# A fused convolution and feed-forward kernel on one core: another order for the same 923 operations

## The chip, the core and the metric

The kernel runs on one NeuronCore of a Trainium2 chip. Five engines work from queues of their own, each strictly in order: TensorE (PE; its weight loads are PEld), VectorE (DVE), ScalarE (ACT), GpSimd (POOL) and SyncE (SP). SP issues transfers only; POOL issues transfers and does small arithmetic. The transfers run on 16 DMA engines that all queues share. The metric is device time in microseconds (us), lower is better.

## The reference

```python
def _A_ref(q, k, v, shift_k, ssm_k, ssm_D):
    ...
    for t in range(ks):                       # 4 taps along the sequence
        k_shift = k_shift + k_pad[:, t:t + S, :] * shift_k[:, ks - 1 - t][None, None, :]
    kv = k_shift * v
    ...                                       # causal convolution of kv with ssm_k by FFT
    y = y + kv * ssm_D[None, None, :]
    return q * y

def _B_ref(x, w_gate, w_up, w_down):
    g = _silu(x @ w_gate)
    u = x @ w_up
    return (g * u) @ w_down

x = A_q
h = x + _A_ref(_layernorm(x, axis=-1), A_k, A_v, A_shift_k, A_ssm_k, A_ssm_D)
h2 = h + _B_ref(_layernorm(h, axis=-1), B_w_gate, B_w_up, B_w_down)
```

The sequence has 2048 positions, the model width is 640, the feed-forward width is 1728, and everything is bfloat16.

## The kernel before

The sequence is cut into four blocks (0 to 3) of 512 positions. The long convolution is done block by block in a frequency domain, and each transform is a set of matrix products. Per block the stages are:

- **Loads.** The filter block g (line 289, from `A_ssm_k`), k (lines 404 and 477), v (line 296), x (line 301, from `A_q`); in block 0 also the transform matrices `WF` (line 903) and `WI` (line 909), the taps (line 889) and the skip weights (line 904).
- **Turning.** g and k are needed with the channels and positions exchanged. Block 0 does it on TensorE (line 411, evicted from PSUM by line 413); later blocks do it with transposing transfers on SP (line 404), for g after a rearranging copy on ScalarE (line 419).
- **kv.** The four taps are small matrix products (line 490); VectorE multiplies by v (line 513 in block 0, line 515 later).
- **Spectra.** Products with `WF` (line 329), evicted from PSUM by line 319 on ScalarE, then sums and differences on VectorE (lines 361 to 396).
- **Products of spectra.** Block j multiplies the spectra X of blocks 0 to j with filter windows H and adds them up: products on VectorE (line 542), sums on VectorE (line 545) or by *adding transfers*, in which the DMA engines read one SBUF tile and add it into another (line 243). Block 3 has the most of these: products with four windows.
- **Inverse.** Sums on VectorE (lines 662 to 677), products with `WI` (line 698), the first layernorm's scale (line 707), gating with x (line 709), the second layernorm's sums (line 606), `rstd` on POOL (line 610).
- **Turning h.** Row tiles (line 722 on ScalarE or 724 on VectorE), turned on TensorE (line 411) or by SP.
- **Feed-forward.** Gate and up products (line 769), silu (line 783), then either a copy on ScalarE (line 785) with a product on VectorE (line 787), or one product on VectorE straight from PSUM (line 786); down products (line 845), and the result added to `out` by an adding transfer (line 852) or stored (lines 754 and 866).

The feed-forward of block j-1 is listed beside the convolution of block j, so that TensorE has matrix products while VectorE works on spectra. Block 3's feed-forward has nothing beside it and runs last.

**What sets the order.** Python code first lists all 923 operations with their reads and writes (`Plan.add`). Then `Plan.run` emits them in the sequence that the hand-given table `ORDER` states (lines 47 to 92), checking that the inputs of each were emitted before. An engine's queue is thus the table, filtered to that engine. A number n stands for operation n; a negative number -n-1 stands for operation n in its second form, on another engine. The forms are these:

```python
evict: ScalarE copy        -> VectorE copy
added: VectorE tensor_add  -> nc.gpsimd.dma_start(..., accum_op=ALU.add)
load:  nc.sync.dma_start   -> nc.gpsimd.dma_start
```

Tiles of the large SBUF arena (22 units) and the four PSUM slots are handed out as `run` goes along, so the table also decides which buffer an operation gets and what it must wait for.

The completion semaphores of transfers are eight per kind of queue, used in turn: the ninth transfer of a queue waits for the landing of the first.

Of the kernel before, what the change touches and what calls it, by code (L numbers as in the profile page):

```python
# [44 lines left out]
UNITS = 22  # L45
SLOTS = {"row": 5, "sg": 3, "ps": 4, "sm": 10}
ORDER = (
# [42 lines left out]
WHOLE = ((0, 1),)  # L90
HB = BLK // 2
DCUTS = ((0, 5), (5, 10), (10, NC_FULL))
# [898 lines left out]
```

## Time and profile before

| what | value |
|---|---|
| time, median of 3 runs | 251.96 us (250.69 to 254.26) |
| profiled execution, span from first to last instruction | 251.4 us |
| median of the runs above the profiled span | 0.56 us |
| PE busy | 237.3 us (94%) |
| DVE busy | 197.7 us (79%) |
| ACT busy | 173.9 us (69%) |
| POOL busy | 54.0 us (21%) |
| DMA queue of SP (hardware_dynamic) | 21.38 MB, 32.1% of the 16 engines' time |
| DMA queue of POOL (software_dynamic) | 11.96 MB, 25.9% |
| granted TensorE clock | 1.000 |

For the profiled execution the page gives the span and no other time; the timed runs are separate executions. "Busy" is the time in which an instruction was executing. The rows quoted in the prediction come from views of the profile: the page itself, the table of stretches of time, the lists of waits, the timeline, the groups by line, and the transfers. In a wait's row the three numbers are total us, times, longest us. In the timeline and in the chain of waits they are start and duration in us. Times of all views are counted from the span's start.

### The profile page before, as it was taken

To read this page: it belongs to the slowest core of one execution; us is meant where nothing else is said; L and a number is where in the kernel's file an instruction comes from. 1 tells how busy PE (TensorE), PEld (TensorE's weight loads), DVE (VectorE), ACT (ScalarE), POOL (GpSimd) and SP (SyncE) were. 2 spreads that over 40 slices of the span, in tenths; PEclk is the share of its full clock that TensorE was granted. 3 is DMA by queue.
4 is the path that set the end of the run, shared out by engine and by line. 5 is a ranking of instruction groups with operands and counts; after the bars stand their busy time and mean duration, and the time that the engine had idled before them with its cause. 6 is when DMAs were issued, how large, how long until landed. Compare 5 with 4: busy or idle time off the path is not lost.

```text
span 251.4 us, 5138 instructions
## 1 busy us (share of the span) xinstructions
PE 237.3 (94%) x2113; PEld 153.0 (61%) x2125; DVE 197.7 (79%) x249; ACT 173.9 (69%) x300; POOL 54.0 (21%) x54
## 2 busy tenths in 40 slices
PE   3869997999999999999999999999999999999994
PEld 3447675788777677444465676454456785465662
DVE  2379999999999999999999989999999542131222
ACT  2449998999999976975988789983542865325100
POOL 0002003231540313220270404263612110000030
PEclk9999999999999999999999999999999999999999
DMA  5995699774998654685345468889592200000052
GB/s 156 376 212 163 127 324 352 231 197 92 165 246 292 202 81 81 105 154 133 79 66 146 86 99 194 148 146 163 98 224 29 26 0 3 0 0 3 0 78 78
DMA packets 37283, 33.66 MB, mean 134 GB/s; under 512 B 22470, under 2 KB 32076, under 8 KB 37260
## 3 DMA queue, kind: packets, MB, share of 16 engines
q1 hardware_dynamic: 31884, 21.38, 32.1%
q0 software_dynamic: 5376, 11.96, 25.9%
q8 instruction: 16, 0.26, 0.4%
q14 instruction: 7, 0.06, 0.1%
HBM read 16.29 MB, written 4.59 MB: 83 GB/s over the span
## 4 chain that ended last, share of the span: by engine, by line
PE 56%; ACT 17%; DMA 10%; DVE 9%; issue 4%; SPq 3%; DVEq 0%; ACTq 0%; POOLq 0%
PE ps L769 24%; PE ps L845 22%; ACT arena L319 7%; DMA arena<-in_A_ssm_k_dram 7%; PE ps L698 5%; DMA arena<-arena 3%; ACT sg L785 2%; PE ps L490 2%; SPq L404 2%; ACT junk L606 1%; PE ps L329 1%; PE ps L833 1%; DVE arena L674 1%; DVE arena L663 1%; DVE arena L662 1%
## 5 line engine op out<-in xcount | busy, mean ns | idle before, releaser
L769 PE MATMUL ps<-arena,wgu 128*128 128x512 bf16 (+1 forms) x668 | 116.7, 328 | 1.4 <-ACT sg L809 0.5
L769 PEld LDWEIGHTS <-wgu 128*128 128x128 bf16 x680 | 66.2, 98 | 45.3 <-issue 1.4
L845 PE MATMUL ps<-wd,tT 128*128 128x320 bf16 x416 | 59.1, 299 | 0.0
L845 PEld LDWEIGHTS <-tT 128*128 128x128 bf16 x416 | 39.8, 98 | 17.2 <-issue 1.8
L542 DVE TENSOR_TENSOR arena<-arena 128x2560 bf16<-128x2560 bf16 x30 | 44.1, 1484 | 0.2
L783 ACT ACTIVATE sg<-ps 128x1024 bf16<-128x1024 f32 (+1 forms) x28 | 26.9, 968 | 20.3 <-PE ps L769 19.7
L329 PE MATMUL ps<-arena,WF 128*128 128x320 bf16 x176 | 29.8, 299 | 1.2 <-ACT arena L319 0.9
L785 ACT CAST sg<-ps 128x1024 bf16<-128x1024 f32 (+1 forms) x23 | 23.0, 998 | 6.9 <-PE ps L769 3.1
L319 ACT CAST arena<-ps 128x320 bf16<-128x320 f32 (+1 forms) x48 | 25.2, 583 | 1.9 <-DVE arena L545 1.1
L610 POOL TENSOR_TENSOR sm<-sm,neghalf 128x4 f32<-128x4 f32 (+1 forms) x10 | 16.6, 1659 | 43.4 <-DVE sm L646 43.1
L787 DVE TENSOR_TENSOR tT<-sg,sg 128x1024 bf16<-128x1024 bf16 (+1 forms) x23 | 15.5, 673 | 11.5 <-ACT sg L785 11.5
L243 POOL DMA_DIRECT2D arena<-arena x11 | 13.3, 1211 | 47.4 <-DVE arena L542 11.2
L329 PEld LDWEIGHTS <-WF 128*128 128x128 bf16 x176 | 17.1, 98 | 10.0 <-issue 2.3
L606 ACT ACTIVATE junk<-arena 128x640 bf16<-128x640 bf16 x28 | 20.8, 744 | 1.3 <-DVE arena L709 1.3
L545 DVE TENSOR_TENSOR arena<-arena 128x2560 bf16<-128x2560 bf16 x14 | 20.7, 1487 | 0.2
L319 ACT ACTIVATE arena<-ps 128x640 bf16<-128x640 f32 (+1 forms) x32 | 20.2, 655 | 0.3
L698 PE MATMUL ps<-arena,WI 128*128 128x320 bf16 x96 | 15.7, 299 | 0.9 <-issue 0.6
L850 ACT ACTIVATE row<-ps,sm 128x640 bf16<-128x640 f32 x12 | 9.5, 791 | 8.2 <-PE ps L845 8.0
L709 DVE SCALAR_TENSOR_TENSOR arena<-arena,sm,ps 128x640 bf16<-128x640 bf16 x16 | 13.6, 876 | 1.8 <-ACT ps L707 1.8
L852 POOL DMA_DIRECT2D out_dram<-row x12 | 11.7, 1153 | 14.1 <-ACT row L850 14.1
L707 ACT ACTIVATE ps<-ps,sm 128x640 f32<-128x640 f32 x16 | 12.1, 770 | 3.7 <-PE ps L698 3.5
L698 PEld LDWEIGHTS <-WI 128*128 128x128 bf16 x96 | 9.0, 97 | 5.6 <-issue 1.3
(91 smaller groups left out, 240.8 us busy)
## 6 DMA issues: line engine op xcount, KB each, us to landing
arena<-arena POOLq DMA_DIRECT2D x11, 640.0 KB, 6.1
arena<-in_A_q_dram SPq DMA_DIRECT2D x4, 640.0 KB, 5.1
out_dram<-row POOLq DMA_DIRECT2D x13, 160.0 KB, 4.2
arena<-in_A_ssm_k_dram SPq DMA_DIRECT2D x3, 640.0 KB, 9.4
arena<-in_A_v_dram SPq DMA_DIRECT2D x3, 640.0 KB, 6.3
wd<-in_B_w_down_dram SPq DMA_DIRECT2D x2, 800.0 KB, 7.3
out_dram<-arena POOLq DMA_DIRECT2D x2, 640.0 KB, 5.8
wgu<-in_B_w_gate_dram SPq DMA_DIRECT2D x1, 800.0 KB, 6.5
```

What stands on the lines that cost most here:

```text
L319: (lambda: nc.scalar.activation(dst(), src(), ACT.Copy, scale=2.0)) if twice else (lambda: nc.scalar.copy(dst(), src())),
L329: nc.tensor.matmul(ap(ps)[:, h, 0:NH], w, ap(src)[:, r, h * NH:(h + 1) * NH], start=(first and i == 0), stop=(last and i == len(rs) - 1), ...
L542: dve(1402, lambda: v.tensor_mul(to(), X.part(xs), H.part(hs)), [X.at(xs), H.at(hs)], [at])
L545: added(1402 * n - 69 * (n - 1), lambda: v.tensor_add(to(), to(), b()), to, b, [what], at, n)
L606: act(725, lambda r=r: nc.scalar.activation(waste(), ap(x)[:, r, :], ACT.Square, scale=D ** -0.5, accum_out=sm(s, MSQ, (r,))), [(x, r)], [ ...
L610: nc.gpsimd.tensor_tensor(sm(s, RSTD, rs), sm(s, VAR, rs), ap(neghalf)[:, 0:len(rs)], op=ALU.pow)
L698: nc.tensor.matmul(ap(ps)[:, w, 0:NH], m, src[:, w * NH:(w + 1) * NH], start=(i == 0), stop=(i == len(terms) - 1))
L769: nc.tensor.matmul(split(ap(ps), n)[:, i, :], w(k), ap(hT)[:, k, lo:lo + n], start=(k == 0), stop=(k == KT - 1))
L783: act(905 if wide_ else 490, lambda: nc.scalar.activation(of(sg), of(*gate), ACT.Silu), [(gate[0], gate[1] + i) for i in range(m)] + (psu ...
L785: op = plan.add("act", 905 if wide_ else 490, lambda: nc.scalar.copy(of(co), of(*up)), psu + [sg], [co] + tt, ("dve", 1135 if wide_ else 6 ...
L787: op.rest = dve(602 if wide_ else 336, lambda: nc.vector.tensor_mul(to(), of(sg), of(co)), [sg, co], tt)
L845: nc.tensor.matmul(ap(ps[hf])[:, hf, 0:NH], ap(tT)[:, c * BLK + at:c * BLK + at + P], ap(wd)[:, c, hf * NH:(hf + 1) * NH], start=False, st ...
```

## The change

Only the table `ORDER` is replaced; all functions stay as they are and their line numbers too. The same 923 operations come in another sequence, and other ones carry a minus sign. With 11 adding transfers before there are 17 now; of plain loads and stores 5 went through POOL's queue, now 21; of evictions 20 were on VectorE, now 26. In detail, nine sums become adding transfers and three go back to VectorE; nineteen plain transfers come to POOL's queue and three go back to SP; twelve evictions come to VectorE and six go back to ScalarE.

```diff
 ORDER = (
-    0, 1, 2, 3, 16, 18, -20, 5, 4, 8, 17, 186, 9, 20, 22, 7, 10, 11, -22, 24, -26, 23, 26, 75, 76, 13, 15, 12, 6,
...
+    0, 16, -18, 8, -16, 3, 1, 9, 5, 10, 18, -20, 7, 26, 2, 11, -187, 20, 21, -13, 22, 24, 23, -26, 75, 76, 6, -14,
...
```

Three places of the program show what that does to the queues.

**SP's queue at the start.** First its rows before, then its rows now (`arena<-in_A_ssm_k_dram` is a filter block, `arena<-arena` a turning of it, `kT` the turned k).

```order
L477 DMA arena<-in_A_k_dram 128x1280
L889 DMA arena<-in_A_shift_k_dram 5x512
L477 DMA arena<-in_A_k_dram 128x1280
L289 DMA arena<-in_A_ssm_k_dram 128x5x512
L296 DMA arena<-in_A_v_dram 128x2560
L903 DMA WF<-const_wf 128x1024
L904 DMA arena<-in_A_ssm_D_dram 1x640
L289 DMA arena<-in_A_ssm_k_dram 128x5x512
L903 DMA WF<-const_wf 128x1024
L301 DMA arena<-in_A_q_dram 128x2560
L909 DMA WI<-const_wi 128x1024 x2
```

```order
L477 DMA arena<-in_A_k_dram 128x1280
L889 DMA arena<-in_A_shift_k_dram 5x512
L296 DMA arena<-in_A_v_dram 128x2560
L404 DMA_TRANSPOSE arena<-arena 128x5x128
L404 DMA_TRANSPOSE kT<-in_A_k_dram 128x5x128
```

SP keeps half of k, the taps and v; it comes to the turning of block 1's g and k after its third transfer, where before all of block 0's loads stood ahead of that.

**POOL's queue at the start**, as a piece of the difference (the rows without a sign stand in both).

```order
+L477 DMA arena<-in_A_k_dram 128x1280
+L904 DMA arena<-in_A_ssm_D_dram 1x16x40
 L872 ISA
 L872 AFFINE_SELECT ident<-ident 128x128
+L289 DMA arena<-in_A_ssm_k_dram 128x5x512 x2
+L903 DMA WF<-const_wf 128x1024 x2
+L301 DMA arena<-in_A_q_dram 128x2560
+L737 DMA wgu<-in_B_w_gate_dram 128x5x640
 L875 MEMSET neghalf 128x4
+L909 DMA WI<-const_wi 128x1024 x2
+L301 DMA arena<-in_A_q_dram 128x2560
 L624 TENSOR_SCALAR sm_76<-sm_76 128x4
```

Eleven transfers stand now ahead of POOL's first layernorm step (line 624): the first of the two filter blocks is block 1's, the second is block 0's, and the gate weights of line 737 are among them.

**POOL's queue during block 3's products of spectra**, before and then now (line 243 is an adding transfer, 852 an addition to `out`, 754 a store of h to `out`; the rows of lines 634 to 610 are block 3's first layernorm, `sm_83`).

```order
L296 DMA arena<-in_A_v_dram 128x2560
L243 DMA arena<-arena 128x2x1280 x3
L634 TENSOR_TENSOR sm_83<-sm_83 128x4
L635 TENSOR_TENSOR sm_83<-sm_83 128x4
L636 TENSOR_SCALAR sm_83<-sm_83 128x4
L610 TENSOR_TENSOR sm_83<-sm_83,neghalf 128x4
L243 DMA arena<-arena 128x2x1280 x2
L852 DMA out_dram<-row_68 128x640
L243 DMA arena<-arena 128x2x1280
L852 DMA out_dram<-row_64 128x640
L852 DMA out_dram<-row_66 128x640
L852 DMA out_dram<-row_65 128x640
```

```order
L243 DMA arena<-arena 128x2x1280
L852 DMA out_dram<-row_67 128x640
L852 DMA out_dram<-row_68 128x640
L243 DMA arena<-arena 128x2x1280
L852 DMA out_dram<-row_64 128x640
L852 DMA out_dram<-row_65 128x640
L243 DMA arena<-arena 128x2x1280 x6
L634 TENSOR_TENSOR sm_83<-sm_83 128x4
L635 TENSOR_TENSOR sm_83<-sm_83 128x4
L636 TENSOR_SCALAR sm_83<-sm_83 128x4
L610 TENSOR_TENSOR sm_83<-sm_83,neghalf 128x4
```

The products of block 3 have eight adding transfers of 640 KB where they had six, and the layernorm step stands now behind the last of them. One sum of block 3 that was an adding transfer earlier in the program (the sum of filter windows, line 466) is back on VectorE.

82 rows, old and new, of the table ORDER are left out of this document.

## The prediction

> **What bounds the kernel now.** I read the totals first, then the table of stretches, then TensorE's waits and its timeline in the stretch that has holes.
>
> ```profile
> span 251.4 us, 5138 instructions
> ...
> PE 237.3 (94%) x2113; PEld 153.0 (61%) x2125; DVE 197.7 (79%) x249; ACT 173.9 (69%) x300; POOL 54.0 (21%) x54
> ```
>
> TensorE (PE) is busy for 237.3 of 251.4 us, so 14.1 us of its idle time are all that an order could ever win. The table of stretches says where they lie (after the stretch's length: busy us of each engine and its instructions, the granted clock, the DMA engines' busy share, GB/s):
>
> ```profile
> core 0: us, PE busy (x) PEld busy (x) DVE busy (x) ACT busy (x) POOL busy (x), PEclk, DMA share, GB/s
> 0.00:15.00 15.00, 7.93 (x174) 5.25 (x175) 5.80 (x16) 4.68 (x4) 0.54 (x6) 1.00 0.94 281
> 15.00:31.00 16.00, 15.97 (x124) 11.26 (x125) 14.92 (x30) 15.28 (x41) 1.88 (x2) 1.00 0.69 137
> 31.00:45.00 14.00, 12.19 (x218) 8.38 (x218) 13.75 (x25) 12.47 (x26) 2.04 (x1) 1.00 1.04 335
> 45.00:68.00 23.00, 22.50 (x204) 19.34 (x203) 22.57 (x21) 22.94 (x40) 6.96 (x5) 1.00 0.69 159
> 68.00:248.00 180.00, 178.72 (x1395) 108.82 (x1406) 140.12 (x160) 118.53 (x193) 42.53 (x41) 1.00 0.51 105
> 248.00:251.40 3.40, 0.00 (x0) 0.00 (x0) 0.53 (x1) 0.00 (x0) 0.00 (x0) 1.00 0.08 24
> ```
>
> The reader is to see 7.1 us of idle PE in the first 15, 1.8 between 31 and 45, 0.5 up to 68, 1.3 in the next 180, and 3.4 after the last product. The granted clock is 1.00 throughout. From 68 us on, PE is the bound, and saving work on another engine there wins nothing. Between 15 and 31 PE counts as busy, but ScalarE (15.28) and VectorE (14.92) are about as full: small products and their evictions keep step.
>
> PE's waits (total us, times, longest) and its timeline at the start name the holes:
>
> ```profile
> PE ps L411 <- DMA arena<-in_A_k_dram: 4.0, 1, 4.0
> PE ps L411 <- DMA arena<-in_A_ssm_k_dram: 3.0, 1, 3.0
> PE ps L329 <- ACT arena L319: 0.9, 1, 0.9
> ```
>
> ```profile
> 6.58 2.44 PE L490 MATMUL ps<-diag,kT 32*128 32x128 bf16 x112
> 8.95 2.68 PE L882 MATMUL ps<-ident 128*128 128x512 bf16 x9
> 11.55 0.43 PE L490 MATMUL ps<-diag,kT 32*128 32x128 bf16 x28
> 14.96 1.03 PE L411 MATMUL ps<-ident,arena 128*128 128x128 bf16 x15 [2.98 <-DMA arena<-in_A_ssm_k_dram]
> 15.82 0.82 PE L329 MATMUL ps<-arena,WF 128*128 128x320 bf16 x4
> ...
> 45.23 1.03 PE L769 MATMUL ps<-arena,wgu 128*128 128x256 bf16 x8 [0.16 <-ACT arena L413]
> ```
>
> PE gets k at 4.0, works until 11.98, and waits 3.0 us for block 0's filter, which lands at 14.91 (row of the chain of waits below). The first spectrum product (line 329) starts at 15.82, the first feed-forward product (line 769) at 45.23.
>
> **The start.** What the loads do together, in two windows, and the chain's row:
>
> ```profile
> 3.90 11.01 DMA arena<-in_A_ssm_k_dram
> ```
>
> ```profile
> DMA packets 2621, 4.22 MB, mean 281 GB/s; under 512 B 391, under 2 KB 1677, under 8 KB 2620
> ...
> q1 hardware_dynamic: 2620, 4.20, 93.2%
> ```
>
> ```profile
> DMA packets 2077, 3.30 MB, mean 367 GB/s; under 512 B 354, under 2 KB 1389, under 8 KB 2076
> ```
>
> The first answer is for 0 to 15 us, the second for 6 to 15. In before all loads stand in SP's queue and the filter lands only when 4.22 MB have moved: x (0.66 MB) and part of `WI` are in that sum, though nothing at 15 us needs them. Now two queues carry them, and block 0's filter and `WF` stand ahead of x in POOL's. What must have moved is k, v and two filter blocks (0.66 MB each) and `WF` (0.52), 3.15 MB. 4.22 − 3.30 = 0.92 MB had moved by 6 us; the other 2.23 at 367 GB/s take 6.1, so the filter is there at about 12.1. PE's own work sets nearly the same time: the warm-up products (line 882) end at 11.6, and in the new order one set of line 411 (0.3 us) and the second line 490 (0.43) follow, then two gatings on VectorE, some 0.4 each, before a spectrum product can read kv. I take 13.1 for the first line 329, 2.7 earlier than 15.82. The bounds are nothing (the loads still interleave) and 3.9 (line 329 directly behind line 490, 11.98).
>
> The row that speaks against it is the 93.2%: the engines were nearly full already. [...]
>
> **From 15 to 45 us.** What ScalarE and VectorE carry here:
>
> ```profile
> L413 ACT COPY arena<-ps 128x640 bf16<-128x640 bf16 x6 | 4.1, 706 | 3.6 <-PE ps L411 3.6
> L319 ACT CAST arena<-ps 128x320 bf16<-128x320 f32 x24 | 9.1, 454 | 0.0
> L606 ACT ACTIVATE junk<-arena 128x640 bf16<-128x640 bf16 x28 | 20.8, 744 | 1.3 <-DVE arena L709 1.3
> L741 ACT COPY wodd<-wgu 128x640 bf16<-128x640 bf16 x1 | 0.7, 742 | 0.0
> ```
>
> One eviction of line 413 (0.71) comes back to ScalarE and one of line 319 (0.45) leaves it: +0.25. One of the steps of 0.74 (a second layernorm square, line 606, or the copy of line 741) stands now ahead of the evictions that free PE's slots; some of it falls into waits, so I charge 0.45. Together −0.7 of the 2.7, and line 769 starts at 43.2: **−2.0**. The gate and up weights, now split over SP and POOL, must be there then. If both waited as k's first half does (4.0), the gain were gone; I charge nothing, since POOL's part is issued ahead of its first layernorm step, over 15 us before.
>
> **From 45 us to block 3.** Six sums fewer on VectorE:
>
> ```profile
> L545 DVE TENSOR_TENSOR arena<-arena 128x2560 bf16<-128x2560 bf16 x14 | 20.7, 1487 | 0.2
> L787 DVE TENSOR_TENSOR tT<-sg,sg 128x1024 bf16<-128x1024 bf16 x22 | 15.1, 685 | 11.5 <-ACT sg L785 11.5
> L786 DVE TENSOR_TENSOR tT<-sg,ps 128x1024 bf16<-128x1024 bf16 x2 | 2.4, 1222 | 6.2 <-PE ps L769 6.2
> ```
>
> 6 × 1.487 = 8.9 us. The evictions cost VectorE something: each of the feed-forward turns 0.685 (line 787) into 1.222 (line 786), +0.54, and the others 0.45 to 0.71; those ahead of block 3's inverse come to about 4.0 by their rows. VectorE has 5.0 less ahead of it there. PE, 178.72 busy of 180, hides that: at most 1.3 could come of it, and I count 0.
>
> **Block 3's adding transfers.** Here the change can lose. In before VectorE is full there, and an adding transfer alone looks like this (window 163.5 to 167.2; then VectorE's stretch; then line 243's time from issue to landing, and its issues):
>
> ```profile
> DMA packets 263, 0.65 MB, mean 176 GB/s; under 512 B 8, under 2 KB 8, under 8 KB 263
> ...
> q0 software_dynamic: 263, 0.65, 98.7%
> ```
>
> ```profile
> 155.80:189.00 33.20, 33.04 (x196) 16.31 (x196) 33.03 (x31) 21.70 (x35) 13.33 (x14) 1.00 0.84 155
> ```
>
> ```profile
> L243 POOL DMA_DIRECT2D arena<-arena x11: 1177/1197/1277, 51.3 to 178.5; - x11
> ...
> DMA to landing us min/median/max: 5.7/6.1/8.1
> ```
>
> One takes the 16 engines 0.987 × 3.7 = 3.65 us. Eight now stand in POOL's queue with four additions to `out` (a quarter of the bytes, 0.9 each): 29.2 + 3.7 + one issue of 1.2 + the last landing's rest (6.1 − 3.65 = 2.4) = 36.5 us. Beside them VectorE has 29 instructions between the last product of line 537 and the last sum of line 582, eighteen of 128x2560 (26.7) and eleven smaller, 34 in all. So it waits 2.5 us for the last sum. It has 5.0 less to do ahead of that, of which 1.4 goes because PE takes block 3's first inverse product one piece of line 845 sooner. 5.0 − 1.4 − 2.5 leaves 1.1: no loss, but little cover. Queued behind the waiting sum are all of VectorE's inverse sums, then PE's line 698 and the whole last feed-forward.
>
> POOL also issues 22 more transfers (six adding, sixteen plain), which at up to 1.2 us each are some 22 us on its 54.0. The layernorm step of block 3 stands behind the eighth addition; its result is first read by the scale of line 707 after the inverse, so it costs nothing before then. Its length depends on VectorE:
>
> ```profile
> 164.48 2.17 POOL L610 TENSOR_TENSOR sm<-sm,neghalf 128x4 f32<-128x4 f32 x1
> 203.69 0.69 POOL L610 TENSOR_TENSOR sm<-sm,neghalf 128x2 f32<-128x2 f32 x1 [4.09 <-DVE sm L646]
> ```
>
> The same step takes 2.17 us beside a full VectorE and 0.69 at the end, where VectorE is mostly idle (half the columns, which alone hardly triples it). [...] The eleven issues of line 243 above, 1.18 to 1.28 us each, lie from 51.3 to 178.5 us, mostly beside a full VectorE, so what the trace shows of it is in my 1.2.
>
> **The end** is unchanged: the last store stays on SP, 3.4 us from the last product.
>
> **The sum.** 251.4 − 2.7 + 0.7 = 249.4 of span. The median of the runs, 251.96, lies 0.56 above the profiled span, so I forecast **249.9**; with the start's gain between its upper bound (3.9) and half of what I take (1.35), 248.7 to 251.3.
>
> **The rivals.**
> - *The start wins nothing.* If the two queues interleave as one did, the filter lands at 14.9 again and ScalarE's extra 0.7 stays: 252.1 + 0.56 = 252.7. For it: the 93.2%. Against it: fewer bytes ahead. Chance 0.2.
> - *Block 3 becomes bound by adding transfers (slower).* Four of the sums hang on each other (the accumulator of lines 545 and 243), and all pass one queue in which VectorE's operands arrive late. It decides from 1.1 / 8 = 0.14 us more per transfer. The landing row runs up to 2.0 over its median; with half of that, 1.0 each, the last sum is 8.0 − 1.1 = 6.9 later, PE stands still for it, and the time is 249.9 + 6.9 = 256.8; with POOL's 1.48 (2.17 − 0.69) on each it is 10.7, 260.6; with 0.4 each, 252.0. Against it: the new order gives VectorE products to do meanwhile. Chance 0.2.
> - *More is won.* If the idle 1.8 us at 31 to 45 and 0.5 up to 68 close too and ScalarE's 0.7 is hidden: 249.9 − 3.0 = 246.9. Against it: SP's transposing transfers and ScalarE are as full there as before. Chance 0.1.
>
> The forecast has 0.5. **Range**: 247.0 to 256.0; below it lies about half of the third rival and a little of the forecast (0.07), above it a bit over half of the second (0.11) and 0.02 for weights that come late. Two per cent is about what a measurement of this kernel tells from no change: faster is below 246.9, slower above 257.0. Faster gets 0.07, slower 0.12 (half of the second rival and the 0.02), within 0.81.
>
> **What the profile would show.** Right: the first line 329 at about 13, the 3.0 us wait for the filter under 1, line 769 at about 43, VectorE near 193 us busy, POOL near 76, a wait of VectorE for `arena<-arena` of 2 to 3 us around line 582, and none of PE at block 3's line 698. Wrong: line 329 at 15 or later (first rival); PE waiting several us for VectorE at line 698 and VectorE for adding transfers before (second); a wait at line 769 for weights, or a later k on PE's first line 411, since half of k now comes by POOL's queue.

## The result, and the profile after

The changed kernel takes 261.43 us (median of 4 runs, 258.73 to 265.55) where the kernel before took 253.09 beside it; the ratio is 1.032, with a 95% interval of 1.023 to 1.042. It is slower, and outside the forecast range. Its profiled execution is the shortest of the four, with a span of 257.0 us:

```profile
span 257.0 us, 5157 instructions
...
PE 239.2 (93%) x2125; PEld 152.7 (59%) x2125; DVE 193.7 (75%) x245; ACT 169.1 (66%) x294; POOL 68.6 (27%) x76
```

VectorE is 4.0 us less busy, as the new forms say, and TensorE's idle time grew from 14.1 to 17.8. The other 1.9 us of the longer span are counted as busy TensorE. Each execution's time lies 1.7 us above its span (258.73 here), so the profiled execution of before would have taken 253.1, more than the median of 251.96 that the forecast went by. Medians below take in every execution, while ratios leave out those over 1.5% longer than the fastest of their kernel, so the two can differ.

I cut every profile at the same products: the first of line 769 (block 0's feed-forward), the first of line 698 (the inverse) of blocks 1, 2 and 3, and the end of the last product. The cuts are where a product is taken up, up to 0.5 us before the start in the timeline. Lengths in us:

| kernel | to 769 | to 698, block 1 | to 698, block 2 | to 698, block 3 | last feed-forward | end | span |
|---|---|---|---|---|---|---|---|
| before | 44.8 | 30.8 | 57.4 | 61.4 | 53.3 | 3.8 | 251.4 |
| after | 44.7 | 31.5 | 60.0 | 61.5 | 54.5 | 4.7 | 257.0 |

About 1.2 us of products are moved from the fourth column to the fifth, so these two count together: 114.65 before and 116.02 now. The 5.6 us are thus nothing at the start, 0.8 in block 1, 2.6 in block 2, 1.4 in block 3 with the last feed-forward, and 0.9 at the end. Of the 1.4, TensorE's idle time makes only 0.2 (0.5 before, 0.7 now); the rest is counted as busy, and the profile doesn't show why. The windows of the first two, before and after (columns as in the forecast's table):

```profile
44.78:75.56 30.78, 30.02 (x260) 24.70 (x259) 29.80 (x30) 30.66 (x52) 10.84 (x8) 1.00 0.77 183
75.56:132.97 57.41, 56.92 (x478) 33.70 (x480) 56.14 (x58) 48.14 (x80) 14.53 (x12) 1.00 0.60 132
```

```profile
44.68:76.22 31.54, 30.02 (x258) 24.38 (x256) 29.79 (x30) 30.08 (x50) 11.52 (x9) 1.00 1.10 261
76.22:136.26 60.04, 57.40 (x481) 33.56 (x482) 55.28 (x60) 45.22 (x76) 16.38 (x15) 1.00 0.74 131
```

In block 2 VectorE was busy for 56.14 of 57.41 us in before: it was as full as TensorE. Now it is busy for 55.28 and idle for 4.8. Its timeline says why, and TensorE's shows the waits that follow:

```profile
95.30 1.49 DVE L542 TENSOR_TENSOR arena<-arena 128x2560 bf16<-128x2560 bf16 x1 [2.50 <-DMA arena<-arena]
...
106.98 1.49 DVE L542 TENSOR_TENSOR arena<-arena 128x2560 bf16<-128x2560 bf16 x1 [0.73 <-DMA arena<-arena]
```

```profile
106.29 4.56 PE L769 MATMUL ps<-arena,wgu 128*128 128x512 bf16 x20 [0.86 <-ACT arena L319]
111.53 19.59 PE L769 MATMUL ps<-arena,wgu 128*128 128x512 bf16 x90 [0.69 <-DVE tT L786]
132.00 3.16 PE L329 MATMUL ps<-arena,WF 128*128 128x320 bf16 x22 [0.89 <-DMA arena<-arena]
```

VectorE waits 2.5 us for the adding transfer of block 2's filter windows, and then everything that hangs on VectorE is late: ScalarE's eviction of line 319 waits 0.8 for VectorE, and the copy of line 419, behind which SP turns the next filter, 0.4. All its waits for adding transfers come to 5.7 us, 4.9 of them in blocks 1 and 2, where before had one of 0.3:

```profile
DVE arena L542 <- DMA arena<-arena: 4.3, 3, 2.5
DVE arena L545 <- DMA arena<-arena: 0.6, 1, 0.6
DVE arena L581 <- DMA arena<-arena: 0.6, 1, 0.6
DVE arena L467 <- DMA arena<-arena: 0.2, 1, 0.2
```

An adding transfer (line 243) now takes 7.1 us from issue to landing, where it took 6.1 (minimum, median, longest):

```profile
DMA to landing us min/median/max: 5.7/7.1/12.4
```

At the start the hole moved instead of closing. TensorE's timeline, and the loads' time from issue to landing:

```profile
8.24 1.25 PE L411 MATMUL ps<-ident,arena 128*128 128x128 bf16 x10 [2.94 <-DMA arena<-in_A_k_dram]
9.43 2.31 PE L490 MATMUL ps<-diag,kT 32*128 32x128 bf16 x112
11.67 2.76 PE L882 MATMUL ps<-ident 128*128 128x512 bf16 x9
...
16.05 3.84 PE L329 MATMUL ps<-arena,WF 128*128 128x320 bf16 x26
```

```profile
arena<-in_A_ssm_k_dram POOLq DMA_DIRECT2D x2, 640.0 KB, 8.2
...
arena<-in_A_k_dram SPq DMA_DIRECT2D x1, 320.0 KB, 3.0
arena<-in_A_k_dram POOLq DMA_DIRECT2D x1, 320.0 KB, 6.9
```

The half of k in POOL's queue lands at 8.2 us; in before it landed at 4.8. Block 0's filter, the second of the two in the first row, is issued at 3.9 and lands 8.7 later, at 12.6, in time. But taps, warm-up and kv now start about 3 us later, and the first line 329 starts at 16.05 instead of 15.82.

### The profile page after: what moved, and what is told of

It reads as the page before. It is cut to its first block, busy times and chain, and to the rows that moved or that the text cites. A ratio compares the mean times of both kernels' runs of the same rounds, so it can differ in the third digit from the quotient of the medians.

```text
span 257.0 us, 5157 instructions
## 1 busy us (share of the span) xinstructions
PE 239.2 (93%) x2125; PEld 152.7 (59%) x2125; DVE 193.7 (75%) x245; ACT 169.1 (66%) x294; POOL 68.6 (27%) x76
## 4 chain that ended last, share of the span: by engine, by line
PE 31%; DVE 26%; DMA 22%; issue 12%; ACT 6%; SPq 1%; POOL 1%; DVEq 0%; POOLq 0%; ACTq 0%
DMA arena<-arena 20%; PE ps L769 12%; PE ps L845 8%; DVE arena L542 7%; PE ps L329 5%; DMA arena<-in_A_k_dram 3%; DVE arena L545 2%; PE ps L698 2%; ACT junk L606 2%; ACT arena L319 2%; DVE tT L787 2%; PE ps L411 1%; DVE arena L709 1%; DVE arena L662 1%; DVE arena L582 1%
## 5 line engine op out<-in xcount | busy, mean ns | idle before, releaser
L845 PE MATMUL ps<-wd,tT 128*128 128x320 bf16 x416 | 60.4, 299 | 0.0
L542 DVE TENSOR_TENSOR arena<-arena 128x2560 bf16<-128x2560 bf16 x30 | 44.2, 1486 | 5.0 <-DMA arena<-arena 4.3
L243 POOL DMA_DIRECT2D arena<-arena x17 | 20.8, 1307 | 72.6 <-DVE arena L542 24.7
L785 ACT CAST sg<-ps 128x1024 bf16<-128x1024 f32 (+1 forms) x19 | 18.4, 967 | 11.7 <-PE ps L769 10.0
L319 ACT CAST arena<-ps 128x320 bf16<-128x320 f32 (+1 forms) x46 | 23.5, 577 | 1.5 <-DVE arena L545 0.8
L319 ACT ACTIVATE arena<-ps 128x640 bf16<-128x640 f32 (+1 forms) x31 | 18.9, 653 | 2.6 <-PE ps L329 2.2
L787 DVE TENSOR_TENSOR tT<-sg,sg 128x1024 bf16<-128x1024 bf16 (+1 forms) x19 | 12.5, 657 | 10.3 <-ACT sg L785 10.3
L786 DVE TENSOR_TENSOR tT<-sg,ps 128x1024 bf16<-128x1024 bf16 (+1 forms) x9 | 9.8, 1099 | 12.2 <-PE ps L769 7.2
L610 POOL TENSOR_TENSOR sm<-sm,neghalf 128x4 f32<-128x4 f32 (+1 forms) x10 | 13.4, 1340 | 20.4 <-DVE sm L646 20.0
L698 PE MATMUL ps<-arena,WI 128*128 128x320 bf16 x96 | 15.9, 299 | 1.6 <-DVE arena L674 0.9
L852 POOL DMA_DIRECT2D out_dram<-row x12 | 12.8, 1178 | 8.0 <-ACT row L850 8.0
L545 DVE TENSOR_TENSOR arena<-arena 128x2560 bf16<-128x2560 bf16 x9 | 13.4, 1488 | 0.7 <-DMA arena<-arena 0.6
```

What stands on the lines that cost most here:

```text
L243: plan.add("dve", ns, fn, reads, [write], ("add", 2 * P * R * D * n, lambda: nc.gpsimd.dma_start(out=to(), in_=what(), accum_op=ALU.add, m ...
L319: (lambda: nc.scalar.activation(dst(), src(), ACT.Copy, scale=2.0)) if twice else (lambda: nc.scalar.copy(dst(), src())),
L542: dve(1402, lambda: v.tensor_mul(to(), X.part(xs), H.part(hs)), [X.at(xs), H.at(hs)], [at])
L545: added(1402 * n - 69 * (n - 1), lambda: v.tensor_add(to(), to(), b()), to, b, [what], at, n)
L698: nc.tensor.matmul(ap(ps)[:, w, 0:NH], m, src[:, w * NH:(w + 1) * NH], start=(i == 0), stop=(i == len(terms) - 1))
L785: op = plan.add("act", 905 if wide_ else 490, lambda: nc.scalar.copy(of(co), of(*up)), psu + [sg], [co] + tt, ("dve", 1135 if wide_ else 6 ...
```

## Experiments

Numbers of `ORDER` name operations; "form" is the engine or queue that the sign selects. The runs differ by some 1.5 us in where the start falls, so stretches say more than totals.

### The new order with one group of forms put back

The half of k on SP (operation 17), all twelve sums, all plain loads and stores, all evictions:

```diff
 e1   -    0, 16, -18, 8, -16, 3, 1,
      +    0, 16, 17, 8, -16, 3, 1,
 e2   sums 218, 262, 442, 482, 489, 684, 688, 691, 699 on VectorE; 645, 679, 703 adding transfers
 e3   nineteen loads and stores on SP, three on POOL
 e4   twelve evictions on ScalarE, six on VectorE
```

> The new order with one sign changed: the half of k that moved to POOL's queue is back on SP's. Theory 1: that half landed at 8.2 us instead of about 4.3, so TensorE had its 3 us hole at 5 to 8 us instead of at 12 to 15, and this alone ate the gain of the earlier filter. Then the first line 329 starts at 13 to 14 us instead of 16.05, line 769 at 43 instead of 45.1, and the time falls by 1.5 to 2.5 us below the changed kernel's. Rival 1: the stretch from 15 to 45 us is bound by something else (evictions, the layernorm of block 0), line 769 starts at 45 again and the time stays. Rival 2: the filter itself lands later, since SP's k now competes: line 329 at 15 to 16.

> The new order with all twelve sums in the form that they had before (nine back on VectorE, three back to adding transfers). Theory 2: the loss behind 45 us comes from VectorE waiting for adding transfers in POOL's queue; then VectorE's waits for them (5.5 us at six places) go, TensorE's idle time from 45 to 200 us falls from about 4.3 to 2, and the time falls by 3 to 6 us. Rival: VectorE is itself the bound in this order; six sums more (8.9 us) make it 3 to 9 us slower.

> The new order with all plain loads and stores on the queues that they had before. Theory 3: the plain loads in POOL's queue hold up adding transfers and the transposing transfers of SP; with them gone the time falls by 3 to 6 us, and the changed kernel's loss is theirs. Rival (adding transfers or evictions are the cause): the time stays within 1.5 us, apart from the start. At the start SP's queue has all loads again, in the new order, with the filter of block 1 ahead: TensorE's hole moves back to 12 to 15 us.

> The new order with all evictions and row scalings on the engines that they had before. Theory 4: the twelve that VectorE took hold up its sums in the wrong places; without them VectorE has 4 us less ahead of block 3's inverse, and the time falls by 2 to 4 us. Rival: ScalarE takes them back and becomes the bound at 15 to 45 us; the time stays or rises by 1 to 2 us.

| kernel | to 769 | to 698, block 1 | to 698, block 2 | to 698, block 3 | last | end | time, ratio to before |
|---|---|---|---|---|---|---|---|
| e1 | 45.6 | 33.3 | 60.0 | 67.3 | 54.6 | 4.7 | 266.9, 1.047 [1.037, 1.058] |
| e2 | 47.6 | 30.8 | 59.9 | 79.0 | 54.7 | 4.8 | 277.5, 1.087 [1.077, 1.097] |
| e3 | 50.8 | 35.2 | 60.1 | 61.2 | 54.5 | 3.8 | 269.5, 1.052 [1.043, 1.062] |
| e4 | 43.9 | 32.8 | 59.7 | 62.3 | 54.7 | 4.7 | 260.9, 1.025 [1.016, 1.035] |

None of the four theories holds as stated: no group put back by itself makes the kernel clearly faster, e2 and, by a hair, e3 make it slower, the intervals of e1 and e4 overlap with the changed kernel's, and block 2 stays at 60 us in all four. In e1 the first line 329 did start earlier, at 14.4 (theory 1: 13 to 14); the gain was gone by line 769. In e2 VectorE is busy for 58.7 of block 2's 59.9 us: the waits are replaced by work of about the same length. In its block 3 VectorE waits for adding transfers again, up to 7.6 us at once.

### Order alone, forms alone

```diff
 e5   the sequence of after, every sign as in before
 f6   the sequence of before, every sign as in after
```

> The new sequence with every sum, load and eviction in the form of before: only the order is changed. Theory 6 (the sequence was made for its own forms, and either half alone is worse than both): block 2's stretch, from block 1's first line 698 to block 2's, stays near 60 us although no sum, load or eviction has moved, and the time is 262 us or more. Rival (the forms are the cause, the sequence is harmless): the stretch falls to 57 to 58 us and the time to 252 to 254.

> The sequence of before with every sum, load and eviction in the form that the change gives it. Theory 6: VectorE reads the sums soon after they are issued, waits for adding transfers in blocks 2 and 3, and the time is 258 to 270 us; block 2's stretch takes 59 us or more. Rival (the sequence is the cause): the stretches stay within 1 us of before and the time at 251 to 254.

e5 took 287.9 us, ratio 1.144 [1.141, 1.146], with block 2 at 64.9; f6 302.5, ratio 1.203 [1.199, 1.206], with block 1 at 41.8 and block 2 at 74.2. VectorE's waits in f6:

```profile
DVE arena L542 <- DMA arena<-arena: 21.1, 4, 7.4
```

Theory 6 holds in its direction, though both losses are far beyond its figures (258 to 270 us for f6, block 2 near 60 in e5): sequence and forms are made for each other, and either half alone loses far more than the change does. That is why putting one group back says little about what it costs in its place.

### Where in the program the loss is

```diff
 h1   before, but from block 1's first line 698 to block 2's: sequence and signs of after
 h2   before up to block 2's first line 698, after from there on
 h3   after up to block 2's first line 698, before from there on
```

> The order and signs of before, but for the stretch from block 1's first line 698 to block 2's, where the order and signs of the change stand (what of it had been issued earlier keeps its place). Theory 2: this stretch alone makes most of the loss, since VectorE is as full as TensorE there and now waits for adding transfers; it takes 59.5 to 60.5 us instead of 57.4, and the time rises by 2 to 3 us. Rival: the stretch only inherits what the earlier blocks lose; it takes 57 to 58 us and the time stays within 1 us.

> Order and forms of before up to block 2's first line 698, and of the change from there on. Theory 7 (block 3's eight adding transfers cost little, as forecast): the stretch to block 3's first line 698 and the last feed-forward take together what they take in before, 114.6 us, within 1.5, the end is 0.9 longer, and the time is 0.5 to 2 us above before. Rival (block 3's adding transfers are the loss): 4 us or more above.

> Order and forms of the change up to block 2's first line 698, and of before from there on. Theory 7: nearly the whole loss is in this part; block 2's stretch takes about 60 us as in the changed kernel, and the time is 3 to 6 us above before. Rival: the time stays within 1.5 us of before, and the loss comes later.

| kernel | to 769 | to 698, block 1 | to 698, block 2 | to 698, block 3 | last | end | time, ratio to before |
|---|---|---|---|---|---|---|---|
| h1 | 43.8 | 31.4 | 62.7 | 64.0 | 53.3 | 3.5 | 263.7, 1.052 [1.045, 1.058] |
| h2 | 43.3 | 30.7 | 57.6 | 62.9 | 54.5 | 3.9 | 258.7, 1.014 [1.010, 1.017] |
| h3 | 44.8 | 31.2 | 61.0 | 61.1 | 53.3 | 3.8 | 257.1, 1.022 [1.020, 1.024] |

h3 carries the larger part of the loss, and in its profile all of it lies ahead of block 2's inverse: behind the cut it takes what before takes. In h2's profile (254.7 us) 2.8 us are added in block 3 with the last feed-forward, more than the 1.5 that theory 7 allowed; the changed kernel has 1.4 there. Of the 2.8, 1.6 are three waits of TensorE for VectorE right behind the cut, which the changed kernel doesn't have. In h1 block 2 alone, with the rest as before, grows by 5.3, more than the 2 to 3 that theory 2 expected:

```profile
94.41 1.49 DVE L542 TENSOR_TENSOR arena<-arena 128x2560 bf16<-128x2560 bf16 x1 [2.67 <-DMA arena<-arena]
...
108.21 1.49 DVE L542 TENSOR_TENSOR arena<-arena 128x2560 bf16<-128x2560 bf16 x1 [2.86 <-DMA arena<-arena]
```

```profile
112.76 19.59 PE L769 MATMUL ps<-arena,wgu 128*128 128x512 bf16 x88 [2.82 <-DVE tT L786]
```

Two waits of VectorE for adding transfers, and one of TensorE for VectorE of about the same length.

### The waits for adding transfers, taken away

s1 leaves all work of VectorE and the order as they are and cuts the five adding transfers that blocks 1 and 2 gained to 64 columns, so their landing is short (the rest of these sums is left out). s3 cuts a sixth, block 3's first new one. g1 puts one of the five on VectorE, g3 the sixth.

```diff
 s1   adding transfers of 218, 262, 442, 482, 489:
-      nc.gpsimd.dma_start(out=to(), in_=what(), accum_op=ALU.add, ...)
+      nc.gpsimd.dma_start(out=to()[:, :, 0:64], in_=what()[:, :, 0:64], accum_op=ALU.add, ...)
 s3   the same for 688 too
 g1   after with 442 on VectorE
 g3   after with 688 on VectorE
```

> The changed kernel, in which the five adding transfers that blocks 1 and 2 gained move 64 of every 640 or 1280 columns; the rest of these sums is left out, VectorE's work and the order stay. Theory 8: VectorE's waits for the landing of these transfers pass straight on to TensorE in blocks 1 and 2; without them its waits for adding transfers fall from 5.5 to under 1.5 us, the stretch to block 1's first line 698 returns to 30.8 us, block 2's to 57 to 58, and the time falls by 2.5 to 4 us. Rival: VectorE has other late inputs behind them (ScalarE's evictions, the filter of block 3); block 2's stretch stays above 59 us and the time falls by less than 1.5.

> The changed kernel with one sign changed: the sum of block 2's filter windows (line 466), which VectorE awaits for 2.5 us at 95 us, is on VectorE again. Theory 8: the wait goes, VectorE works 1.5 us more, and block 2's stretch falls from 60.0 to about 59 us; the time falls by 0.5 to 1.5. Rival: another input is late there and the stretch stays at 60 or grows by the 1.5.

> The kernel with the five shrunk sums, and a sixth cut to 64 of 1280 columns: block 3's first adding transfer that the change added, issued within 1 us of the turnings of block 2's rows on SP. Theory 9 (this transfer takes the engines ahead of the last turning, which then lands 7.6 us after its issue instead of about 3, and TensorE waits 4.0 us for it): the wait goes, block 3's stretch falls from 67.0 to 62 to 63 us, and the time falls from 258.3 to 253.5 to 255. Rival (the additions to out or the turnings themselves are slow): the wait stays at 3 us or more and the time within 1 us.

> The changed kernel with that one sum on VectorE again, nothing left out. Theory 9: in the profiled execution of the changed kernel the last turning came in time, in the others (1.9 to 6.8 us longer) it did not; without the transfer beside it all executions are near the shortest: a median of 257.5 to 259.5 instead of 261.4, with VectorE 1.5 us busier. Rival: the spread has another cause; the median stays at 261 or more.

Blocks 1 and 2 in s1:

```profile
44.43:74.33 29.90, 29.45 (x257) 24.47 (x256) 29.68 (x30) 29.44 (x49) 10.84 (x9) 1.00 0.99 247
74.33:131.48 57.15, 56.76 (x484) 33.73 (x482) 55.13 (x60) 45.49 (x77) 16.26 (x14) 1.00 0.57 104
```

```profile
DVE arena L542 <- DMA arena<-arena: 0.9, 1, 0.9
```

Both stretches are back at or below before's length, 1.6 and 2.9 us under the changed kernel's, and VectorE's waits for adding transfers fall from 5.7 to 0.9. s3, which has the same five cut, repeats it (29.9 and 57.1), while block 2 takes 60.0 to 61.5 in the other profiles that have the changed kernel's forms there (after, e1, g2, g3, h3). Theory 8 holds, with one limit: a short transfer also takes less of the DMA engines (a busy share of 0.57 in block 2, 0.74 in the changed kernel), so s1 doesn't tell the landing time from the load. The time fell to 258.3, but its ratio of 1.026 [1.021, 1.031] is not clear of the changed kernel's, because a wait that the changed kernel's profile doesn't have came in block 3:

```profile
158.81 1.50 PE L769 MATMUL ps<-arena,wodd 128*128 128x256 bf16 x10 [3.99 <-DMA arena<-row]
```

This is the turning of block 2's rows on SP. The last of the four is issued at 151.15, 0.7 us behind the start of the issue of block 3's first new adding transfer at 150.42. Its time from issue to landing in s1 (window 151.1 to 159), and that of the same turning in after (155.2 to 163):

```profile
arena<-row SPq DMA_TRANSPOSE x1, 7.5
```

```profile
arena<-row SPq DMA_TRANSPOSE x1, 3.2
```

In after the distance was smaller (155.29 behind 155.19), and the turnings came in time. The other profiles with both issues fall in line: 0.2 us behind in h2, no wait; 0.4 in e1, 0.6 in g1 and 0.8 in g2, waits of 3.7, 3.9 and 4.5 us. s3 decides it: with that transfer short the wait is 0.7,

```profile
PE ps L769 <- DMA arena<-row: 0.7, 1, 0.7
```

block 3's stretch falls from 67.0 to 62.2, and the time to 255.3, ratio 1.014 [1.009, 1.020]. g3, with nothing left out, took 258.8 (258.1 to 260.6), ratio 1.027 [1.022, 1.032], where the changed kernel itself spreads up to 265.6. Both agree with theory 9, though g3's interval overlaps with the changed kernel's. The longer executions of the changed kernel have no traces, but g2 (below) is the same program up to its last four stores, and its profiled execution, 9.1 us longer, shows this wait and another one in block 1:

```profile
68.45 1.49 DVE L581 TENSOR_TENSOR arena<-arena 128x2560 bf16<-128x2560 bf16 x1 [3.11 <-DMA arena<-arena]
```

```profile
79.21 0.99 PE L698 MATMUL ps<-arena,WI 128*128 128x320 bf16 x4 [3.64 <-DVE arena L674]
...
168.22 2.27 PE L769 MATMUL ps<-arena,wodd 128*128 128x256 bf16 x10 [4.50 <-DMA arena<-row]
```

So the spread, too, comes at least in part from waits for transfers: block 1 with the changed kernel's sequence and forms takes from 31.2 to 42.6 us in six profiles (after, e1, g1, g2, g3, h3), and with those of before 30.7 to 30.8 in six (before, f1, f2, f3, h2, s2). With all six transfers short some 3 us remain (s3): against before's profile 0.7 to line 769, 2.1 in block 3 with the last feed-forward and 1.0 at the end, less 1.2 in blocks 1 and 2.

g1 took 262.8, ratio 1.034 [1.027, 1.042], no different from the changed kernel: theory 8's fall of the time didn't come. Its profiled execution was the longest (272.7), with longer waits in block 1 than the other profiles of the same sequence and forms have there (VectorE 6.6 us for an adding transfer, TensorE 5.5 for a turning of the filter; e1 has the latter with 2.4). But in block 2 the wait of 2.5 us is gone, and the stretch takes 58.7, where theory 8 expected about 59:

```profile
86.27:144.95 58.68, 56.92 (x484) 33.70 (x482) 56.13 (x60) 45.62 (x77) 14.68 (x13) 1.00 0.61 117
```

That is only one profile, but nothing of the kernel's work is left out in it.

### The start

```diff
 f1   before, with 12, 13, 14, 15, 27, 28, 29 (filter, WF, skip weights, x, WI) on POOL's queue
 f2   f1 and 17 (half of k) on POOL's queue
 s2   before, with 28 and 29 (WI) behind 192 in SP's queue, and 31 and 33 (line 912) later on VectorE
```

> The order of before, with block 0's filter, both halves of WF and of WI and block 0's x on POOL's queue; k, taps, v and block 1's filter stay on SP's. Theory 1 (the bytes ahead of the filter decide): the filter lands at 11 to 13 us, the first line 329 starts at 13 to 14.5 instead of 15.8, and the time falls by 1 to 2.5 us. Rival (the queues share 16 full engines and interleave): k lands later, the filter at 14 to 15, and the time stays within 1 us.

> As the run before it, and half of k on POOL's queue too, as in the change. Theory 1b: that half lands at 5 to 7 us instead of 4.3, TensorE's first turning waits 1 to 3 us longer, and the first line 329 moves back by as much; the time is 1 to 3 us above that of the kernel without this move. Rival: TensorE's warm-up products take up the delay, no difference.

> The order of before, with the two loads of WI (0.52 MB) behind the first turning of block 1's filter and block 1's x in SP's queue, and the two steps that read WI later on VectorE. Theory 1c (the bytes that share the engines with the filter decide when it lands, on whichever queue): 0.52 MB fewer, 1.4 us at 367 GB/s, so the filter lands about 1 us earlier than in before and the time falls by 0.5 to 1.5 us. Rival: TensorE's warm-up ends no earlier and ScalarE's evictions up to 45 us take the gain; the time stays within 0.5 us.

f1 took 256.3 us, ratio 1.016 [1.011, 1.021]; f2 253.4, 1.008 [1.005, 1.010]; s2 255.6, 1.011 [1.004, 1.018]. None starts line 329 early (16.5, 16.1 and 15.9). TensorE and VectorE in f1:

```profile
6.84 1.25 PE L411 MATMUL ps<-ident,arena 128*128 128x128 bf16 x10 [1.44 <-DMA arena<-in_A_k_dram]
...
14.73 0.44 PE L411 MATMUL ps<-ident,arena 128*128 128x128 bf16 x5 [1.32 <-DVE arena L513]
```

```profile
13.39 3.15 DVE L513 TENSOR_TENSOR arena<-ps,arena 128x512 bf16<-128x512 f32 x6 [4.77 <-DMA arena<-in_A_v_dram]
```

k's second half comes at 6.8 instead of 4.8 although it stayed on SP, and v at 13.4 instead of 11.1: up to 15 us POOL's queue takes 40.4% of the 16 engines' time and SP's 48.6%, where SP's had 93.2% in before, and k and v on SP's are late. So theory 1 (bytes ahead of the filter decide) is wrong as I put it. So is theory 1b: in f2 k's second half came 1.0 us later still, but v 0.4 earlier, and with it line 329. In s2 fewer bytes move up to 15 us (3.91 MB, 4.22 in before), but TensorE then waits 2.1 us for VectorE's gating with v (line 513), where it had waited for the filter: the next input was as late. (In before this gating ends at 14.28, 0.6 us ahead of the filter, so an earlier filter alone had no more than that to win.) Line 912, which I moved, then held up line 698 by 2.2. The rivals named the right mechanism for f1 (k later), but no rival expected f1 and s2 to lose more than 1 us.

The same start as in before lies in h1, h2 and the kernel f3 below, and there the first line 329 comes at 14.2, 13.8 and 14.3. The 15.8 of the first profile was a late one. In these four profiles line 769 begins at 43.3 to 44.8 us, 43.8 on average; in the five with the changed kernel's start (after, g1, g2, g3, h3) at 43.7 to 45.3, 44.7 on average. So the change loses about 0.9 us at the start, which the first two profiles hide.

### The end

```diff
 f3   before, with 907, 912 and 922 (last stores) on POOL's queue and 902 on SP's
 g2   after, with these four as in before
```

> The order of before, with the last stores on the queues that the change gives them (three of the last rows on POOL's, one earlier row on SP's). Theory 5: the end from the last product to the span's end grows from 3.8 to 4.7 us, since POOL's transfers land 0.8 us later than SP's; the time rises by about 0.9. Rival: the end stays at 3.8, and the longer end of the changed kernel is from something else.

> The changed kernel with the last stores on the queues of before. Theory 5, after the run in which before got the new queues and its end did not grow: the end depends on what the last POOL transfer is in this order; with SP alone the end is 3.8 us instead of 4.7, and the time falls by about 0.9. Rival: the end stays at 4.7.

f3 took 251.6 us, ratio 1.000 [0.997, 1.003], with an end of 3.6. g2 spread from 256.5 to 267.8, too much for a comparison; its end is 3.7. So in the new order the end is 3.7 to 3.8 with SP's stores (e3, e5, g2) and 4.7 to 4.8 with POOL's, but h2 has POOL's stores and an end of 3.9. What makes the 0.9 us is open.

No kernel tried here beats the one before.

## Why the prediction was wrong

- **The start, −2.7.** Wrong: +0.2 in the profile, and line 769 begins about 0.9 later over all profiles. The sum over bytes was near (filter at 12.1, measured 12.6), and so was the way from the warm-up to line 329 (1.5 us, measured 1.6). The step that failed is "the warm-up products (line 882) end at 11.6": they ended at 14.4. I left k at its old landing time although half of it had moved to POOL's queue; the prediction names "a later k" among the signs of being wrong and gives it no price. It came at 8.2 instead of 4.8, and TensorE's 7.8 us of serial work behind it set the start. The first rival's outcome (nothing won) came true, and f1 agrees with it: with loads moved to POOL's queue, the two queues shared the 16 engines' time up to 15 us (40.4% and 48.6%), and k's second half and v came 2.0 and 2.3 us later.
- **15 to 45 us, +0.7.** Mis-sized: from line 329 to line 769 it took 29.1 us, where it was 29.4. No extra cost showed.
- **45 us to block 3, "I count 0".** This is the step that cost most. I took TensorE's 178.72 of 180 us as proof that VectorE's time is covered there. It was not: in block 2 VectorE was busy for 56.14 of 57.41 us, so both were bounds, and there a wait of VectorE has no cover. I priced the sums saved (8.9 us) and not the waits for their landing; those were 5.7 us, 4.9 of them in blocks 1 and 2. Without these transfers' landing and load the 0.8 and 2.6 us are gone (s1, s3).
- **Block 3's adding transfers.** The forecast of a 2.5 us stall and 1.1 to spare was on the safe side: VectorE's waits there come to 0.6. What makes block 3 and the last feed-forward 1.4 longer is open.

```profile
188.81 1.49 DVE L545 TENSOR_TENSOR arena<-arena 128x2560 bf16<-128x2560 bf16 x1 [0.61 <-DMA arena<-arena]
```

  The second rival's mechanism, a wait for adding transfers, was the right one, at the wrong place: it named block 3, and it struck in blocks 1 and 2 (4.9 us of waits), where fewer adding transfers stand but VectorE reads each soon after. What I did not name at all is an adding transfer that delays SP's turning of rows, 3.7 to 4.5 us where it strikes (s1 against s3 for the cause). The trace of before has those turnings on SP from 145.9 to 151.3 us, just ahead of its first adding transfer of block 3's products (153.3), so the collision could have been looked for.
- **The end, "unchanged".** Wrong by 0.9 us, cause open.
- **Busy times.** VectorE's 193.7 (forecast 193) was right; POOL rose by 14.6, where 22 were forecast. The engines' totals told nothing of the loss.
- **From span to time, +0.56.** Too small: an execution's time lies 1.7 above its own span. The profiled execution was slower than the median that it was set against, which hid 1.1 us.
- **The rest.** The third rival (more is won at 31 to 68 us) did not come: TensorE's idle time there was 2.3 and is 2.8. The range ended at 256.0, since the slower rival was priced for one place and every other place was held at nothing or better.

## What to carry to other kernels

Before an engine's time is called covered, look at the busy share of each engine in the stretch itself: where two are full (here 56.92 and 56.14 of block 2's 57.41 us), a wait of either one can go straight to the end. Work that moves from an engine to a transfer frees its duration but puts the landing time (here 6 to 7 us for 1.5 us of VectorE) ahead of the next reader, so look in the order for who reads it and when. Transfers that are put on a second queue can also delay the ones left on the first (in f1 k's second half came at 6.8 us instead of 4.8): list what lands in the same microseconds, on all queues.

## What the runs showed of the hardware

In two traces a long wait of TensorE cost more than its length. The hole of 4.0 us in s1 and the stretches behind it:

```profile
154.80:158.80 4.00, 0.03 (x1) 0.02 (x1) 2.45 (x2) 2.00 (x5) 2.65 (x3) 1.00 1.10 137
158.80:162.00 3.20, 3.19 (x15) 1.85 (x16) 0.10 (x1) 1.59 (x5) 0.31 (x1) 0.64 1.13 210
162.00:164.00 2.00, 2.00 (x10) 0.98 (x8) 2.00 (x3) 1.71 (x4) 0.00 (x0) 0.73 1.11 187
164.00:166.00 2.00, 2.00 (x11) 0.88 (x9) 2.00 (x2) 1.94 (x4) 0.00 (x0) 1.00 0.17 30
```

The granted clock falls to 0.64 and 0.73 for 5.2 us, which adds 0.36 × 3.2 + 0.27 × 2.0 = 1.7 us, an estimate from these rows that takes the products to slow down with the clock. Five of them (line 769, 128x512) take 2.34 us from 160.10 on, and 1.24 in after, where there is no such wait and the clock is 1.00. In e2 a wait of 6.1 us is followed by a clock of 0.50 for 5.7 us:

```profile
204.20:210.30 6.10, 0.00 (x0) 0.00 (x0) 4.03 (x5) 0.00 (x0) 0.00 (x0) 0.66 0.35 62
210.30:213.00 2.70, 2.69 (x12) 1.08 (x13) 2.67 (x2) 0.79 (x1) 0.84 (x1) 0.50 0.00 0
213.00:216.00 3.00, 3.00 (x13) 1.72 (x12) 2.93 (x4) 0.00 (x0) 0.09 (x1) 0.50 0.48 55
```

The 2.98 us of before left it at 1.00 (14.96 to 18.00 us).

At the start the clock column reads 1.00, and the prediction took it so, but the first products behind the 4.0 us without any take twice their later time in before. The 112 products of line 490 that begin at 6.58 take 2.44 us (a row in the prediction); in block 3 of the same trace they take

```profile
151.33 1.18 PE L490 MATMUL ps<-diag,kT 32*128 32x128 bf16 x112
```

At 11.55 the next 28 take 0.43, as they do later on (0.43 at 37.88, 95.91 and 156.61). In after the 112 take 2.31 at 9.43, so TensorE's work behind the late k was partly slow work.

And a turning transfer landed 3.2 us after its issue in after, where it is issued 0.1 us behind an adding transfer on POOL's queue, and 7.5 in s1, where it is issued 0.7 us behind; with that adding transfer short (s3), the stretch to block 3's line 698 is 4.8 us shorter than in s1.
